# A bound on the transfers in flight in a scan followed by a mixture of adapters

## The chip, the cores and the metric

The kernel runs on one core of a Trainium2 chip. The metric is the device time of one execution in microseconds, as the median of several runs. The profile is of one further execution; its span runs from the first to the last instruction.

## The reference

There are two parts. The first is a linear recurrence over time, for 8 sequences of 6,400 steps with 128 channels: `h = a[:, t] * h + b[:, t]`, and every `h` is kept. The second takes the 51,200 rows of the result, `x`, and adds a mixture of low-rank adapters to each:

```python
logits = x @ w_gate                      # 8 experts
topk = the two largest logits of a row   # w = softmax over these two
delta = sum over both: w * ((x @ A[e]) @ B[e])   # A[e]: 128 x 16, B[e]: 16 x 128
out = x + delta
```

All inputs and outputs are float32. `a` and `b` are 26.2 MB each and are read once; the output is 26.2 MB and is written once.

## The kernel before

The 51,200 rows are cut into 100 units of 512 rows. One unit goes through these steps:

- **Load** (`load`, L533, issued at L350 by SyncE). Rows of `a` and of `b` come in transfers of 512 KB, two units each; the first one of `a`, the first two of `b` and the last one of `a` are single units of 256 KB. Each of the two inputs has a ring of 8 places (`a_in`, `b_in`).
- **Transpose** (`AB`, L571). TensorE turns the rows into channels by time, into PSUM.
- **Scan** (L605, L629). ScalarE copies the transposed `a` to SBUF (`a_st`), and VectorE scans it with the transposed `b`, into `xT` in float16.
- **Products and gates** (`ZL` L668, `zl` L686, and L735 to L824). TensorE multiplies `xT` by the gate weights and all the `A` at once, ScalarE parks the result, and VectorE, GpSimd and ScalarE find the two largest logits and their weights, for three units at a time.
- **Weighting and output** (`mul` L845, `T` L853, `tev` L861, `D` L881, `oev` L896). The products are weighted, turned, multiplied by `B` and added to `x` in PSUM; ScalarE copies the sum into one of 24 output slots (`outt`).
- **Store** (`store`, L913, also issued at L350 by SyncE). Two units, 512 KB, go out in one transfer; the last two units go out singly.

SyncE does nothing but issue these 153 transfers: 51 of `a`, 51 of `b` and 51 stores. The order of the work on every engine is written out ahead by a planner, `_Plan.schedule`. It takes each operation's cost, a key (unit plus an offset for its kind) and its dependencies, and fills `self.order`, one list for each engine. A store has the key of 20 units later (`hold`) and also depends on the scan of that later unit, so that stores are mixed with the loads from the 41st transfer on. After planning, `_Plan.run` walks an engine's list: it waits on semaphores for what the operation depends on (L194), then emits it. Each DMA has a semaphore of its buffer place and counts to 16, one for each DMA engine that has done its part.

Before the change, a transfer waits only for its buffers: a load for the transposes that last read its place, a store for its two units' `oev` and the later scan. Beyond that, SyncE issues as early as it can.

Of the kernel before, what the change touches and what calls it, by code (L numbers as in the profile page):

```python
# [12 lines left out]
CFG = {  # L13
    "ring": 8,
    "xr": 20,
    "zr": 48,
    "nout": 24,
    "hold": 20,
    "heads": (1, 1, 1, 1),
    "group": 3,  # L20
    "tails": (2, 2, 1, 1),
# [20 lines left out]
class _Op:  # L42


    def __init__(self, name, eng, kind, unit, busy, lat, emit, deps, dma, mode, takes, gives):
        self.name = name
        self.engs = (eng,) if isinstance(eng, str) else eng
        self.eng = self.engs[0]
        self.kind = kind
        self.unit = unit  # L50
        self.busy = busy if isinstance(busy, dict) else {e: busy for e in self.engs}
        self.lat = lat
        self.emit = emit
        self.deps = deps
        self.dma = dma
        self.mode = mode
        self.takes = list(takes)
        self.gives = gives
        self.next = None
        self.turn = None  # L60
        self.signal = False
        self.done = None


class _Plan:


    def __init__(self, sems, latency, weight, offset, switch, banks, caps, least):
        self.sems = sems
        self.latency = latency  # L70
        self.weight = weight
        self.offset = offset
        self.switch = switch
        self.banks = banks
        self.caps = caps
        self.least = least
        self.ops = {}
        self.order = {e: [] for e in sems}
        self.bank_of = {}
# [10 lines left out]
    def schedule(self):  # L90
        ops = self.ops
        users = {n: [] for n in ops}
        left = {}
        glued = {op.next for op in ops.values() if op.next}
        for op in ops.values():
            op.deps = [ops[d] for d in dict.fromkeys(op.deps) if d in ops]
            left[op.name] = len(op.deps)
            for d in op.deps:
                users[d.name].append(op)
            op.key = self.weight * (op.unit + self.offset.get(op.kind, 0.0))  # L100
        end = {}
        cand = {e: [] for e in self.sems}
        free = {e: 700.0 for e in self.sems}
        link = 0.0
        mode = None
        idle = [(0.0, i, None) for i in range(self.banks)]
        held = {r: 0 for r in self.caps}
        for op in ops.values():
            if not left[op.name] and op.name not in glued:
                for e in op.engs:  # L110
                    cand[e].append((0.0, op))
        todo = len(ops)
        turn = 0
        while todo:
            best = None
            for e, c in cand.items():
                for x in c:
                    op = x[1]
                    if op.turn is not None and op.turn != turn:
                        continue  # L120
                    t = max(free[e], x[0])
                    takes = op.takes + (ops[op.next].takes if op.next else [])
                    if takes:
                        want = {}
                        for r, _ in takes:
                            want[r] = want.get(r, 0) + 1
                        kept = sum(max(0, k - held[r] - want.get(r, 0)) for r, k in self.least.items())
                        if len(takes) + kept > len(idle) or any(held[r] + k > self.caps[r] for r, k in want.items()):
                            continue
                        t = max(t, idle[len(takes) - 1][0])  # L130
                    if op.mode and mode and op.mode != mode:
                        t += self.switch
                    late = op.busy[e] - min(op.busy.values())
                    if best is None or (t + late, op.key) < best[:2]:
                        best = (t + late, op.key, e, x, t)
            _, _, e, pick, t = best
            for x in pick[1].engs:
                cand[x].remove(pick)
            run = [pick[1]] + ([ops[pick[1].next]] if pick[1].next else [])
            for op in run:  # L140
                for role in op.takes:
                    _, i, giver = idle.pop(0)
                    self.bank_of[role] = i
                    held[role[0]] += 1
                    if giver and giver.eng != e:
                        run[0].deps.append(giver)
            for op in run:
                turn += op.turn is not None
                op.eng = e
                mode = op.mode or mode  # L150
                self.order[e].append(op)
                free[e] = t + op.busy[e]
                t = free[e]
                if op.dma:
                    link = max(link, free[e] + 550.0) + op.dma[2]
                    end[op.name] = link + op.dma[3]
                else:
                    end[op.name] = free[e] + op.lat[e]
                if op.gives:
                    held[op.gives[0]] -= 1  # L160
                    idle.append((end[op.name], self.bank_of[op.gives], op))
                    idle.sort(key=lambda x: x[:2])
                todo -= 1
                for u in users[op.name]:
                    left[u.name] -= 1
                    if not left[u.name] and u.name not in glued:
                        for x in u.engs:
                            cand[x].append((max(end[d.name] for d in u.deps), u))
        self.span = max(end.values())
        for op in ops.values():  # L170
            if op.eng == "pe":
                op.deps = [d for d in op.deps if d.eng != "pe"]
            for d in op.deps:
                d.signal = True
        for e, seq in self.order.items():
            n = 0
            for op in seq:
                if op.dma:
                    op.done = op.dma[:2]
                else:  # L180
                    n += op.signal
                    op.done = (self.sems[e], n)
# [18 lines left out]
def bass_associative_scan_2x2__then__mixture_of_adapters_kernel(  # L201
# [28 lines left out]
    KEY = CFG["key"]  # L230
# [59 lines left out]
    with ExitStack() as stack:  # L290
# [38 lines left out]
        psum = [sb(nc.psum_tensor(f"ps{i}", [128, UT], F32)) for i in range(8)]  # L329
# [4 lines left out]
        sems = {e: sb(nc.semaphore(f"s_{e}")) for e in ("pe", "dve", "act", "pool", "sp")}  # L334
        dma_sem = {}

        latency = {"pe": 205.0, "dve": 170.0, "act": 230.0, "pool": 130.0, "sp": 100.0}
        plan = _Plan(sems, latency, 1000000.0, KEY, 100.0, len(psum), CFG["caps"], CFG["least"])
        add = plan.add

        def add_dma(name, eng, unit, starts, slot, ns, deps=(), kind="dma", issue=450.0, after=2000.0):
# [105 lines left out]
        for name, eng, lo, hi, time in (("spr0", "pool", 0, 3, 900.0), ("spr1", "dve", 3, 8, 760.0)):  # L447
# [10 lines left out]
                    op=ALU.mult,  # L458
# [549 lines left out]
```

## Time and profile before

| | |
|---|---|
| time | 202.24 us, median of 3 runs (202.14 to 203.49) |
| span of the profiled execution | 200.8 us |
| busy: PE, PEld, DVE, ACT, POOL | 90%, 80%, 87%, 89%, 79% |
| moved by DMA | 79.30 MB, mean 395 GB/s |
| a 512 KB transfer, from issue to landing | median 15.2 to 15.4 us |
| mean granted TensorE clock | 0.988 |

PE is TensorE's matmuls, PEld its weight loads, DVE VectorE, ACT ScalarE, POOL GpSimd, SP SyncE; a q behind the name (SPq) stands for the engine's sequencer, which waits and issues. Lines of groups and waits name the tile, the line of the kernel and what was waited for, with the total in us, the number of times and the longest. In the stretches of time the columns are the stretch, its length, the busy time of each engine with its number of instructions, the granted clock, the mean busy share of the 16 DMA engines and GB/s. "Issue" as a cause of waiting means that the profile shows nothing the engine waited for.

### The profile page before, as it was taken

How to read it: one execution, taken by the hardware profiler on the slowest of the kernel's cores; microseconds unless marked ns; L12 is line 12 of the kernel's file. 1: busy time of each engine (PE TensorE's matmuls, PEld its weight loads, DVE VectorE, ACT ScalarE, POOL GpSimd, SP SyncE). 2: the span in 40 equal slices, each digit the busy share in tenths (PEclk: the TensorE clock that was granted, in tenths of full speed). 3: DMA queues.
4: the chain of work that ended last, by engine and by line, in shares of the span. 5: the costliest groups of instructions: out<-in, count | busy, mean ns of one | idle time of the engine just before them, and what ended most of it. 6: DMA issues, size and time to landing. Idle time of an engine off the chain costs nothing.

```text
span 200.8 us, 8186 instructions
## 1 busy us (share of the span) xinstructions
PE 181.6 (90%) x3202; PEld 161.6 (80%) x3202; DVE 174.3 (87%) x302; ACT 179.6 (89%) x463; POOL 158.4 (79%) x278
## 2 busy tenths in 40 slices
PE   7688899997997999999899999999999999989671
PEld 4577788897996888889788999888989889979461
DVE  4389999999899998899998989879889799889980
ACT  3379999999897999999899999999999999999872
POOL 2234749889696988897859999999899998897850
PEclk9889999999999999999999999999999999999998
DMA  6999999999999999999999999999999999985997
GB/s 206 367 419 410 406 409 404 412 403 406 408 418 414 417 412 417 411 417 416 411 414 419 411 415 415 419 415 415 417 417 412 413 415 415 406 340 202 371 406 276
DMA packets 22629, 79.30 MB, mean 395 GB/s; under 512 B 2624, under 2 KB 2880, under 8 KB 22592
## 3 DMA queue, kind: packets, MB, share of 16 engines
q1 hardware_dynamic: 22160, 78.65, 97.6%
q8 instruction: 25, 0.41, 0.8%
q10 hardware_dynamic: 432, 0.14, 0.3%
q14 instruction: 12, 0.10, 0.1%
HBM read 52.56 MB, written 26.21 MB: 392 GB/s over the span
## 4 chain that ended last, share of the span: by engine, by line
PE 47%; DVE 18%; ACT 14%; DMA 7%; issue 6%; SPq 4%; POOL 2%; POOLq 1%; DVEq 0%; ACTq 0%
PE ps L571 17%; PE ps L881 15%; DVE xT L629 13%; PE ps L668 8%; DMA b_in<-in_b_dram 7%; PE ps L853 7%; ACT a_st L605 4%; ACT zl L686 4%; ACT outt L896 4%; SPq L350 4%; DVE zwT L861 2%; ACT pn L735 1%; ACT g L824 1%; DVE zw L845 1%; POOLq L290 1%
## 5 line engine op out<-in xcount | busy, mean ns | idle before, releaser
L629 DVE TENSOR_TENSOR_SCAN xT<-a_st,xT,ps 128x512 f16<-128x512 f32 x96 | 120.4, 1254 | 12.5 <-PE ps L571 4.5
L845 POOL TENSOR_TENSOR zw<-zl,g 128x512 f16<-128x512 f32 x93 | 99.2, 1071 | 10.2 <-ACT g L824 10.1
L686 ACT COPY zl<-ps 128x408 f32<-128x408 f32 (+1 forms) x139 | 74.6, 543 | 1.6 <-PE ps L668 1.4
L571 PE MATMUL ps<-ident_f,a_in 64*128 64x64 f32 (+1 forms) x792 | 68.3, 230 | 4.9 <-DMA a_in<-in_a_dram 2.4
L605 ACT COPY a_st<-ps 128x512 f32<-128x512 f32 x100 | 62.2, 641 | 8.8 <-PE ps L571 8.0
L571 PE MATMUL ps<-ident_f,b_in 64*128 64x64 f32 (+1 forms) x792 | 68.3, 231 | 1.8 <-issue 1.7
L571 PEld LDWEIGHTS ps<-ident_f,a_in 64*128 64x128 f32 (+1 forms) x792 | 57.1, 140 | 14.5 <-issue 5.2
L896 ACT COPY outt<-ps 128x512 f32<-128x512 f32 x100 | 61.8, 633 | 3.2 <-PE ps L881 2.7
L571 PEld LDWEIGHTS ps<-ident_f,b_in 64*128 64x128 f32 (+1 forms) x792 | 57.1, 141 | 1.2 <-issue 1.0
L668 PE MATMUL ps<-cst_h,xT 128*128 128x136 f16 x400 | 50.3, 234 | 0.8 <-DVE xT L629 0.7
L881 PE MATMUL ps<-ident_h,xT 128*128 128x128 f16 x400 | 42.1, 228 | 1.0 <-DVE zwT L861 0.8
L853 PE MATMUL ps<-ident_h,zw 128*128 128x128 f16 x400 | 38.9, 220 | 3.9 <-DVE zw L845 2.0
L881 PE MATMUL ps<-cst_h,zwT 128*128 128x128 f16 x400 | 39.0, 219 | 1.4 <-issue 1.4
L668 PEld LDWEIGHTS ps<-cst_h,xT 128*128 128x128 f16 x400 | 36.2, 148 | 4.6 <-DVE xT L629 1.5
L861 DVE COPY zwT<-ps 128x256 f32<-128x256 f32 x89 | 35.8, 411 | 3.2 <-PE ps L853 3.2
L881 PEld LDWEIGHTS ps<-ident_h,xT 128*128 128x128 f16 x400 | 32.9, 146 | 3.0 <-DVE zwT L861 1.9
L853 PEld LDWEIGHTS ps<-ident_h,zw 128*128 128x128 f16 x400 | 25.0, 98 | 9.0 <-DVE zw L845 3.0
L881 PEld LDWEIGHTS ps<-cst_h,zwT 128*128 128x128 f16 x400 | 27.2, 99 | 0.4 <-issue 0.4
L735 ACT ACTIVATE pn<-d 128x96 f32<-128x96 f32 (+2 forms) x72 | 23.6, 336 | 1.0 <-POOL d L777 0.6
L785 POOL TENSOR_TENSOR L<-zl,pn 128x96 f32<-128x96 f32 (+2 forms) x34 | 12.9, 378 | 6.9 <-ACT pn L735 5.7
L807 POOL TENSOR_TENSOR d<-d 128x96 f32<-128x96 f32 (+2 forms) x36 | 13.8, 383 | 4.3 <-DVE d L760 3.9
L814 POOL TENSOR_TENSOR um<-d,pn 128x96 f32<-128x96 f32 (+2 forms) x36 | 14.0, 388 | 2.8 <-ACT pn L735 1.4
(40 smaller groups left out, 87.7 us busy)
## 6 DMA issues: line engine op xcount, KB each, us to landing
a_in<-in_a_dram SPq DMA_DIRECT2D x49, 512.0 KB, 15.4
b_in<-in_b_dram SPq DMA_DIRECT2D x49, 512.0 KB, 15.3
out_dram<-outt SPq DMA_DIRECT2D x49, 512.0 KB, 15.2
a_in<-in_a_dram SPq DMA_DIRECT2D x2, 256.0 KB, 9.0
b_in<-in_b_dram SPq DMA_DIRECT2D x2, 256.0 KB, 4.4
out_dram<-outt SPq DMA_DIRECT2D x2, 256.0 KB, 2.9
cst_f<-in_moe_A_dram ACTq DMA_DIRECT2D x1, 64.0 KB, 3.2
cst_f<-in_moe_B_dram ACTq DMA_DIRECT2D x1, 64.0 KB, 5.8
```

Of the source, the lines that this page charges most:

```text
L571: last = h.transpose(*args())
L605: lambda h: h.copy(a_st[w % NAS][:, :], bank(("a", w))[:, :]),
L629: last = h.tensor_tensor_scan(out=x_at(lo, hi), data0=a_st[w % NAS][:, lo:hi], data1=bank(("b", w))[:, lo:hi], initial=init, op0=ALU.mult, ...
L668: last = h.matmul(dst, x_block((b0 + j) // Q, (b0 + j) % Q), wA_h)
L686: return h.copy(zl[:, r0 : r0 + n, :], src)
L735: lambda h: h.activation(v(pn[s]), v(src[s]), ACTF.Relu, bias=bias, scale=scale),
L814: lambda h: h.tensor_tensor(out=v(um[s]), in0=v(d1[s]), in1=v(pn[s]), op=ALU.subtract),
L845: lambda h: h.tensor_tensor(out=oview, in0=zview, in1=gview, op=ALU.mult),
L853: last = h.transpose(dst[:, q * 128 : (q + 1) * 128], zw[v % NZW][:, q, :], ident_h[:, :])
L861: return copy(zwT[v % NZT][:, :].bitcast(F32), bank(("O", v))[:, 0 : UT // 2])
L881: last = h.matmul(bank(("O", v))[:, cols], (x_block(v, q), zwT[v % NZT][:, cols])[part], (ident_h[:, :], Bcat_h)[part], start=part == 0 an ...
L896: return copy(outt[:, v % NOUT, :], bank(("O", v))[:, :])
```

## The change

After the planner has settled the order, every transfer of SyncE's list also gets a dependency on the one four places earlier in the same list. SyncE then waits, before it issues a transfer, until that earlier one has landed, so that at most four are in flight, the new one included. The order of the transfers, their sizes, the buffers and all that the other engines do stay as they were. It is meant to keep the queues of the DMA engines short, in place of the twelve or so transfers that stand in them now.

```diff
@@ CFG
     "hold": 20,
+    "flight": 4,
@@ _Plan.__init__
+        self.flight = flight
@@ _Plan.schedule
         self.span = max(end.values())
+        moves = [op for op in self.order["sp"] if op.dma]
+        for old, new in zip(moves, moves[self.flight :]):
+            new.deps.append(old)
         for op in ops.values():
             if op.eng == "pe":
                 op.deps = [d for d in op.deps if d.eng != "pe"]
```

`flight` is handed to the planner where it is made (L338).

More of the change, by code (lines that the diff above doesn't have):

```diff
@@ L65, with __init__ @@
 class _Plan:
-    def __init__(self, sems, latency, weight, offset, switch, banks, caps, least):
+    def __init__(self, sems, latency, weight, offset, switch, banks, caps, least, flight):
         self.sems = sems
@@ L337, in bass_associative_scan_2x2__then__mixture_of_adapters_kernel @@
         latency = {"pe": 205.0, "dve": 170.0, "act": 230.0, "pool": 130.0, "sp": 100.0}
-        plan = _Plan(sems, latency, 1000000.0, KEY, 100.0, len(psum), CFG["caps"], CFG["least"])
+        plan = _Plan(sems, latency, 1000000.0, KEY, 100.0, len(psum), CFG["caps"], CFG["least"], CFG["flight"])
         add = plan.add
```

## The prediction

> **What bounds the kernel now.** I read the page's slices and queue rows first, to see whether the DMA engines have room to lose:
>
> ```profile
> DMA  6999999999999999999999999999999999985997
> q1 hardware_dynamic: 22160, 78.65, 97.6%
> q8 instruction: 25, 0.41, 0.8%
> a_in<-in_a_dram SPq DMA_DIRECT2D x49, 512.0 KB, 15.4
> b_in<-in_b_dram SPq DMA_DIRECT2D x49, 512.0 KB, 15.3
> out_dram<-outt SPq DMA_DIRECT2D x49, 512.0 KB, 15.2
> ```
>
> They have almost none: 97.6% of sixteen engines' time is SyncE's queue. In the trace's landings one 512 KB transfer follows another every 1.25 to 1.28 us, so 15.3 us from issue to landing is 15.3 / 1.26 = 12 transfers in flight. SyncE's timeline shows how the twelve come about:
>
> ```profile
> 9.15 0.43 SPq L350 DMA_DIRECT2D a_in<-in_a_dram  x1
> 9.63 0.43 SPq L350 DMA_DIRECT2D b_in<-in_b_dram  x1
> 10.10 1.98 SPq L350 DMA_DIRECT2D a_in<-in_a_dram  x1
> 12.13 1.05 SPq L350 DMA_DIRECT2D b_in<-in_b_dram  x1
> ```
>
> An issue takes 0.43 us until the queue is full; from 10 us on it takes 1 to 3 us, because the sequencer is stuck inside it. The buffers don't hold SyncE back, the queue does.
>
> Does a late load cost anything? The chain of waits, for the whole span and then from 30 to 185 us:
>
> ```profile
> PE ps L571 <- DMA a_in<-in_a_dram: 2.4, 3, 1.5
> ...
> PE ps L571 <- DMA a_in<-in_a_dram: 0.2, 1, 0.2
> ```
>
> TensorE waits for loads only before 30 us. Up to unit 19 its transposes start 0.05 to 1.2 us after the later of their two loads has landed; from unit 31 on they start 4.7 to 9.7 us after (unit 60: landed 100.43, started 105.83). From then on the busy time by stretches sets the pace (PE, PEld, DVE, ACT, POOL):
>
> ```profile
> 40.00:160.00 120.00, 114.12 (x2112) 104.12 (x2111) 108.74 (x181) 114.40 (x290) 107.64 (x182) 1.00 1.03 414
> 160.00:175.00 15.00, 15.00 (x266) 13.59 (x266) 14.06 (x25) 14.77 (x38) 13.40 (x24) 1.00 1.03 414
> ```
>
> TensorE and ScalarE are busy 95% from 40 to 160 us and 98 to 100% after it. So two resources run level: DMA, 5 us ahead, and TensorE with ScalarE. What still interrupts TensorE is in the list of waits and in the chain that ended last:
>
> ```profile
> PEld ps L571 <- issue: 6.2, 17, 1.2
> PE ps L571 <- issue: 1.7, 2, 1.0
> PE ps L881 <- issue: 1.4, 2, 1.2
> ...
> 49.18 1.04 issue
> 62.94 1.17 issue
> 99.14 0.66 issue
> ```
>
> "Issue" is a wait for nothing that the profile names. Counting TensorE's instructions in the trace, these three stops come after instructions 1473, 1985 and 3265, which are 2 and 5 times 256 apart, and each follows a packet of the q8 instruction queue (47.73 to 48.83, 61.55 to 62.52, 97.41 to 98.48 us). They are stops for TensorE's own program.
>
> **What the Trainium skill says.** "Runtime: NRT & Kernel Launch", section Instruction fetch mechanics: the program is streamed in blocks of 16 KiB, 256 instructions, over a DMA queue that the sequencer drives, and mostly hidden. The trace agrees on the blocks (25 packets, 0.41 MB, is 16 KB each, for 6,404 TensorE instructions) and not wholly on "hidden". "DMA: Bandwidth & Descriptors", Queues, rings and completion order: an engine takes turns between its queues packet by packet. The trace agrees in that a fetch takes about 1.0 us beside two data packets stretched from 0.16 to about 0.44 and 0.38 us. Same page, Anatomy of one DMA: a transfer has a fixed cost near 2.0 us, mostly the receipt. Here a lone 256 KB store lands after 2.9 us; less 0.63 us of moving, that leaves 2.3 us, but the trace puts more of it at the start than at the receipt (below). Same page, Why a DMA increments its semaphore by 16 and not by 1: only the full count says that all engines are done, so the added wait is one for the slowest engine. The sixteen landings of a transfer lie 0.4 us apart at 3 us, 2.9 at 30, 4.1 at 90 and 6.6 at 175.
>
> **The change, part by part.** It adds 149 waits on SyncE (153 transfers less four). It moves no instruction and keeps the order; no other engine gets a wait.
>
> *The wait itself.* Behind the waiting SyncE are only later transfers, so the question is whether the engines run dry. From an engine's last packet to the visible landing the trace has 0.35 to 0.50 us. SyncE's wake-up is not shown; I take 0.1 us, twice the 0.05 us between two free issues (ends 0.05 and 0.3). From issue to the first data packet: 1.0 us for the first load (0.74 to 1.74), 0.75 us for stores near the end (183.35 to 184.1). Round trip: 0.45 + 0.1 + 1.0 = 1.55 us. Meanwhile the slowest engine still holds three transfers, 3 x 1.26 = 3.8 us. It never runs dry; 2.2 us are spare. The end of the run supports this: from 188 to 198 us, with two to four others in flight, stores still land every 1.23 to 1.39 us. Cost: 0.
>
> *The other waits.* A transfer would be issued some 10 us later than now, so its buffer waits (loads on transposes, stores on scans) are older when it gets there: 0. Only the last stores, held for the last scans until 183.35 and 185.34 us, keep today's issue times.
>
> *Coupling the engines.* Now an engine that loses 1.5 us to a fetch (1.0 plus 0.5 of stretched packets; landings at transfers 11 and 57 jump by 1.5) falls behind alone, up to 6.6 us. After the change no engine can be over 2.2 us ahead of the slowest. One fetch fits in that; a second one on the same engine, before the slowest has had one too, costs 2 x 1.5 - 2.2 = 0.8 us. With 24 fetches on 16 engines I reckon six such cases at most, 5 us; the least is 0. The slowest engine has its own jumps in any case (three of 1.1 to 1.5 us now), each of which gives all others room again, so I take 1 us. That lies beside the 4.7 us that loads are early, and 5.3 us between a store's landing and the reuse of its output slot (unit 80: 163.60 and 169.01). At the end the stores leave about 1 us of gaps. Cost on the end: 0 to 4, taken 0.3 us.
>
> *The fetches.* A fetch starts 2.5 to 5.3 us after TensorE has entered the block before. It needs 1.0 us, and TensorE goes on no sooner than 1.3 us after its end. The stops of 1.04, 1.17 and 0.66 us belong to starts after 5.1 to 5.3 us; at 2.5 to 3.5 us there is no stop. Part of that delay should be the data packets that the engine has already taken in. Now about 12 x 8 = 96 packets stand at an engine; after, 32 at most (5 us), and on an engine that leads by 2.2 us about 18. Gain if fetches start 1.4 us sooner: all the stops at block ends, 1.04 + 1.17 + 0.66 + 0.4 of smaller ones = 3.3 us, nearly all on the chain. If the delay isn't the queue: 0. I take half, 1.6 us, since the slowest engines keep some 28 packets.
>
> Sum: 202.24 + 0.3 - 1.6 = 200.9 us.
>
> **The rivals.** *Nothing happens*: the fetches' delay is their own, the engines' order is the same. For it: packets are shared in turns, so depth alone need not matter. 202.24 + 0.3 = 202.5. *All stops go*, and the early stretch gains too: before unit 20 every load is waited for, transfers 2 and 3 land 1.7 us later than the rate allows, and transfer 11 loses 1.5 us to a fetch. With fewer transfers issued at once some of that may not occur: 202.24 + 0.3 - 3.3 - 0.5 = 198.7. Against it: transfers 2 and 3 are issued as before. *Coupling wins*: fetches fall on leading engines and the spare 2.2 us is smaller under load, so SyncE adds bubbles; 5 us of delay, less 1 us of gaps, gives 202.24 + 4 = 206.2, the case that is slower. Against it: the round trip is measured on both sides, and most of the middle is hidden.
>
> **How the numbers follow.** Forecast 0.44, nothing 0.20, all stops 0.20, coupling 0.16. A forecast that lies 0.7 us above the mark of 1% (200.2) falls below it in somewhat over a third of its cases: faster 0.20 + 0.17 = 0.37. Slower by 1% (over 204.3) is the coupling and a remnant of "nothing": 0.17. The rest, 0.46, is within 1%. The range runs from the whole stop gain, 198.8, to half-way into the coupling case, 204.8.
>
> **What would show it.** Right: time from issue to landing near 5 us for all three kinds; issues of 0.4 us; DMA still 9 in the slices up to 175 us; a transfer's sixteen landings never over about 2.3 us apart; shorter "issue" waits of L571. Wrong towards slower: slices of DMA at 7 or 8 in the middle, waits of L571 on a_in after 40 us, loads ending well after 176 us. Wrong towards no effect: the 1 us "issue" stops still there. A first load phase that ends at another time than before would mean that I mis-sized the start.

## The result, and the profile after

The kernel with the bound takes 221.88 us (median of 4 runs, 218.67 to 224.09) against 202.31 us before: ratio 1.083, 95% interval 1.074 to 1.092. The forecast was 200.9 us, range 198.8 to 204.8. The kernel is slower, and by some four times the 4 us that my slower rival allowed. (Two of the four runs count as slow, so the ratio rests on the other two, 218.67 and 219.94 us, and is below 221.88 / 202.31.)

Of the page before, the GB/s of the slices and the chain that ended last, by engine:

```profile
GB/s 206 367 419 410 406 409 404 412 403 406 408 418 414 417 412 417 411 417 416 411 414 419 411 415 415 419 415 415 417 417 412 413 415 415 406 340 202 371 406 276
...
PE 47%; DVE 18%; ACT 14%; DMA 7%; issue 6%; SPq 4%; POOL 2%; POOLq 1%; DVEq 0%; ACTq 0%
```

The page of the changed kernel, first the slices (DMA busy in tenths, GB/s), then the chain, then the transfers with their time from issue to landing:

```profile
DMA  5999999999999999989999999999999999999995
GB/s 203 377 402 349 348 397 376 364 383 368 373 361 390 350 381 305 387 305 354 393 373 392 376 376 366 386 311 394 367 340 373 383 376 374 377 390 401 400 406 219
...
DMA 55%; PE 17%; ACT 10%; DVE 7%; issue 3%; POOL 3%; POOLq 1%; SPq 1%; DVEq 0%
...
a_in<-in_a_dram SPq DMA_DIRECT2D x49, 512.0 KB, 5.6
b_in<-in_b_dram SPq DMA_DIRECT2D x49, 512.0 KB, 5.6
out_dram<-outt SPq DMA_DIRECT2D x49, 512.0 KB, 5.5
```

The bound does what it says: 5.6 us to landing, three others in flight at every issue. But look at its first two lines together. The engines still read 9 in nearly every slice, while the bytes that they move fall below 380 GB/s in many of them. The busy share hides most of this loss, because a packet that takes longer counts as busy for longer (such packets are counted below); GB/s shows it. The chain, which led through DMA for 7% of the span before, is now 55% DMA. By stretches (columns as before):

```profile
0.00:40.00 40.00, 33.14 (x499) 26.32 (x501) 31.62 (x53) 28.69 (x76) 18.58 (x44) 0.96 0.93 350
40.00:160.00 120.00, 109.08 (x1997) 99.54 (x1995) 104.11 (x171) 110.00 (x277) 103.69 (x175) 0.99 0.99 365
```

From 40 to 160 us it is 365 GB/s in place of 414, while the busy share falls only from 1.03 to 0.99 (above 1, the packets overlap a little in the record). And TensorE waits for loads again, all through the run; the list of waits of the changed kernel (L576 is L571 of before) has:

```profile
PEld ps L576 <- DMA b_in<-in_b_dram: 12.0, 16, 2.7
PEld ps L576 <- DMA a_in<-in_a_dram: 11.6, 16, 1.6
PE ps L576 <- DMA b_in<-in_b_dram: 9.1, 12, 2.5
PE ps L576 <- DMA a_in<-in_a_dram: 8.3, 14, 1.4
```

The landings in the trace tell where the time went. The last load lands at 193.76 us in place of 175.96, 17.8 us later, and the last store at 217.62 in place of 200.25, 17.4 later. From transfer 4 to 132 there are 128 intervals between landings. Those that are more than 0.1 us above 1.26 us are above it by 23.0 us in sum, in 36 intervals, in place of 5.5 us in 12. So it isn't a slower steady rate: 85 of the 128 still last between 1.20 and 1.36 us, and 36 jumps make up the loss. The loads' lead over TensorE still grows to 7 us at unit 34, but is eaten up by unit 47, which starts 0.2 us after its load; from there on the loads set the pace.

### The profile page after: what moved, and what is told of

It is laid out like the page before. It is cut to its first block, busy times and chain, and to the rows that moved or that the text cites. A ratio compares the mean times of both kernels' runs of the same rounds, so it can differ in the third digit from the quotient of the medians.

```text
span 218.2 us, 8276 instructions
## 1 busy us (share of the span) xinstructions
PE 184.4 (85%) x3202; PEld 163.1 (75%) x3202; DVE 175.8 (81%) x302; ACT 182.0 (83%) x463; POOL 158.8 (73%) x278
## 4 chain that ended last, share of the span: by engine, by line
DMA 55%; PE 17%; ACT 10%; DVE 7%; issue 3%; POOL 3%; POOLq 1%; SPq 1%; DVEq 0%
DMA b_in<-in_b_dram 27%; DMA a_in<-in_a_dram 23%; PE ps L576 7%; DMA out_dram<-outt 5%; DVE xT L634 5%; PE ps L886 5%; ACT zl L691 3%; PE ps L673 3%; PE ps L858 3%; ACT outt L901 3%; ACT a_st L610 2%; ACT pn L740 1%; POOL zw L850 1%; DVE zw L850 1%; POOLq L295 1%
## 5 line engine op out<-in xcount | busy, mean ns | idle before, releaser
L576 PE MATMUL ps<-ident_f,a_in 64*128 64x64 f32 (+1 forms) x792 | 69.8, 230 | 19.0 <-DMA b_in<-in_b_dram 9.1
L576 PEld LDWEIGHTS ps<-ident_f,a_in 64*128 64x128 f32 (+1 forms) x792 | 57.2, 140 | 30.5 <-DMA b_in<-in_b_dram 12.0
L610 ACT COPY a_st<-ps 128x512 f32<-128x512 f32 x100 | 60.9, 619 | 19.9 <-PE ps L576 18.7
L691 ACT COPY zl<-ps 128x408 f32<-128x408 f32 (+1 forms) x139 | 71.2, 520 | 1.0 <-PE ps L673 0.9
L576 PE MATMUL ps<-ident_f,b_in 64*128 64x64 f32 (+1 forms) x792 | 69.8, 230 | 0.1
L901 ACT COPY outt<-ps 128x512 f32<-128x512 f32 x100 | 60.3, 614 | 3.5 <-PE ps L886 2.3
L576 PEld LDWEIGHTS ps<-ident_f,b_in 64*128 64x128 f32 (+1 forms) x792 | 57.1, 140 | 0.3 <-issue 0.2
L886 PE MATMUL ps<-ident_h,xT 128*128 128x128 f16 x400 | 42.6, 230 | 0.7 <-DVE zwT L866 0.6
L858 PE MATMUL ps<-ident_h,zw 128*128 128x128 f16 x400 | 39.8, 224 | 3.2 <-DVE zw L850 2.1
L886 PEld LDWEIGHTS ps<-ident_h,xT 128*128 128x128 f16 x400 | 33.4, 147 | 2.3 <-DVE zwT L866 1.4
L858 PEld LDWEIGHTS ps<-ident_h,zw 128*128 128x128 f16 x400 | 25.8, 100 | 6.7 <-DVE zw L850 3.1
L740 ACT ACTIVATE pn<-d 128x96 f32<-128x96 f32 (+2 forms) x72 | 22.1, 314 | 0.7 <-POOL d L782 0.6
L812 POOL TENSOR_TENSOR d<-d 128x96 f32<-128x96 f32 (+2 forms) x36 | 13.7, 381 | 3.7 <-DVE d L765 3.2
```

What stands on the lines that cost most here:

```text
L576: last = h.transpose(*args())
L610: lambda h: h.copy(a_st[w % NAS][:, :], bank(("a", w))[:, :]),
L691: return h.copy(zl[:, r0 : r0 + n, :], src)
L740: lambda h: h.activation(v(pn[s]), v(src[s]), ACTF.Relu, bias=bias, scale=scale),
L858: last = h.transpose(dst[:, q * 128 : (q + 1) * 128], zw[v % NZW][:, q, :], ident_h[:, :])
L886: last = h.matmul(bank(("O", v))[:, cols], (x_block(v, q), zwT[v % NZT][:, cols])[part], (ident_h[:, :], Bcat_h)[part], start=part == 0 an ...
```

## The experiments

**How far the bound has to be loosened.** Only the number is changed.

```diff
-    "flight": 4,
+    "flight": 5,
```

> All 148 added waits stay, only the bound is five in place of four. Theory A (round trip): from the changed kernel's trace a new transfer reaches an idle engine 0.36 us (receipt) + 0.06 us (wake-up) + about 2.1 us (issue to first packet) = 2.5 us after the slowest engine finished the transfer it waited for, so an engine can be ahead of the slowest by (flight - 1) x 1.26 - 2.5 us: 1.3 us at four, less than the 1.5 us that an instruction fetch costs an engine; 2.5 us at five. Fetches are mostly absorbed again: 203 to 209 us. Theory B (the waits themselves on SyncE cost time, whatever their distance): still 216 to 222 us. Theory C (every transfer that is issued later lands later, in proportion to the depth given up): a fall by about 2 to 3 us for each step of flight, 217 us.

Measured: 203.38 us, ratio to the kernel before 1.003 (1.001 to 1.006).

> Bound six. Theory A: an engine may be 3.8 us ahead, two fetches' worth: 200 to 204 us. If the shorter stops for instructions are worth something by themselves, it shows here: up to 3 us under the kernel before. Theory B: 216 to 222 us. Theory C: about 214 us.

Measured: 202.67 us, ratio 1.001 (0.998 to 1.003).

> Bound eight. Theory A: 6.3 us ahead, no fetch is felt: 199.5 to 203 us. Theory B: 216 to 222 us. Theory C: about 209 us.

Measured: 203.38 us, ratio 1.003 (1.001 to 1.005).

> Bound twelve, about what the queue holds by itself: the waits are all there and hardly ever hold SyncE. Theory A and C: the time of the kernel before, 201 to 203.5 us. Theory B: 216 to 222 us.

Measured: 203.49 us, ratio 1.003 (1.000 to 1.005).

One transfer more gives back nearly all of the 8%. The added waits cost about 0.3% (B falls: with five, 140 of the 148 held transfers are still issued within 0.1 us of the landing that they waited for), and there is no slope from depth to time (C falls). The page of the kernel with a bound of five:

```profile
GB/s 212 381 418 411 400 363 405 405 404 404 408 416 410 411 419 413 398 394 413 405 408 408 414 412 410 406 407 418 398 383 381 390 408 391 416 412 383 409 392 161
...
a_in<-in_a_dram SPq DMA_DIRECT2D x49, 512.0 KB, 6.4
```

Mostly above 400 again with 6.4 us to landing. These runs also answer the question of the stops for instructions. The "issue" pieces in the chain of the kernel with a bound of six, the longest of its first 100 us:

```profile
48.17 1.18 issue
62.07 1.17 issue
...
98.55 0.69 issue
```

They come at nearly the same times as before and are about as long (1.04, 1.17 and 0.66 us there), at half the depth. With five there are two of them, 0.91 and 1.17 us. With four none is longer than 0.7 us, but there TensorE is held up by loads, so that it can reach the ends of its blocks later.

**The transfers by themselves.** To see whether four is too few by itself, the compute is left out: SyncE walks the same list, waiting only for the transfer `flight` places back (the stores write zeros), and TensorE either does nothing or streams matmuls on a constant tile, which makes it fetch program and nothing else.

```diff
-            plan.run("sp", h)
+            plan.moves_only(h, ready)
...
+            for i in range(CFG["stream"]):
+                h.matmul(psum[i // 16 % 8][:, 0:128], warm_t[:, 0:128], warm_t[:, 0:128])
```

> Only SyncE's 153 transfers in their order, bound of four, no buffer waits; all compute is left out (stores write zeros), so TensorE fetches no program. Theory A (a bound of four is too tight only because fetches displace single engines): nothing pushes engines apart, three transfers' work (3.8 us) covers the round trip of 2.5 us, landings 1.26 to 1.28 us apart, 193 to 198 us. Rival D (four in flight is by itself too few for this round trip, fetches or not): landings on average 1.38 us apart, 210 to 218 us.

Measured: 205.54 us.

> The same with a stream of 3,202 TensorE matmuls on a constant tile, which fetch as many program blocks as the kernel's and wait for nothing. Theory A: 24 or so fetches of 1.5 us on engines that lead by no more than 1.3 us: the 0.5 to 0.9 us lost at each come back, 207 to 216 us, with a jump of the landings at each fetch. Rival D: as without the stream, within 3 us.

Measured: 219.75 us, about the whole kernel's time with a bound of four (218.67 and 219.94 us), with none of its compute.

> The same stream with the bound at twelve. Theory A: fetches fall on engines that may lead by more than 10 us, only the unluckiest engine's own count: 195 to 201 us. Rival D: the same, 195 to 201 us; but then the gap to four without the stream is as large as to four with it.

Measured: 199.89 us. With four in flight the fetches add 219.75 - 205.54 = 14.2 us; with fetches, the step from twelve to four costs 219.75 - 199.89 = 19.9 us. But moves alone came 7.5 us above the most that I had expected of them, so a control was needed:

> Moves only, no stream, bound of twelve: the control for moves only at four (205.5 us). Theory A in its strict form (only program fetches push engines apart): 195 to 198 us, and the 8 to 10 us between it and four have another cause, such as slow single packets that are seen in the trace of four after 60 us (0.3 to 2.2 us each). If those slow packets occur here too and cost nothing, the coupling is to any loss on one engine, not to fetches alone. Rival D: no such packets here, 195 to 198 us as well, but then the difference to four is spread evenly over the transfers.

Measured: 195.89 us. Thus four costs 9.6 us even without program fetches, and theory A in its strict form falls. (The two ran on different chips; the kernel before took 202.98 us on the one and 204.00 on the other, which is small beside 9.6.) The stretches of moves only with four, then with twelve (the last column is GB/s):

```profile
10.00:40.00 30.00, 3.93 (x1) 0.00 (x0) 1.00 1.02 405
60.00:170.00 110.00, 0.00 (x0) 0.00 (x0) 1.00 1.00 382
```

```profile
10.00:40.00 30.00, 3.93 (x1) 0.00 (x0) 1.00 1.03 411
60.00:170.00 110.00, 0.00 (x0) 0.00 (x0) 1.00 1.03 419
```

With loads alone and no fetches four in flight is nearly enough: from 20 to 50 us the trace has a landing every 1.25 to 1.30 us, but for one of 1.47. Stores are issued from 50 us on, and after that there are jumps of up to 2.5 us, so rival D (too few always, spread evenly) falls as well. What the jumps consist of shows in the 4 KB packets. At the line rate one takes 0.159 us; this counts those over 0.3 us after 12 us of each trace, and what they took above 0.159 us, summed over all engines:

| kernel | packets over 0.3 us | excess, us |
|---|---|---|
| before | 58 | 14.5 |
| changed, four | 492 | 218.5 |
| five / six / eight | 144 / 81 / 58 | 55.8 / 26.1 / 15.0 |
| moves only, twelve | 2 | 0.4 |
| moves only, four | 243 | 121.6 |
| moves and fetches, twelve | 42 | 10.8 |
| moves and fetches, four | 528 | 246.9 |

In the changed kernel 218.5 us over 16 engines is 13.7 us for each, against 0.9 before. The slow packets, up to 2.1 us long, aren't program fetches; they are data packets, and nearly all such packets are quick when twelve transfers stand in the queue. The remainder is engines with nothing to do: from 12 to 193 us fewer than 16 packets are under way in 26% of the time, 5.3 us for each engine, where before, from 12 to 175 us, it is never so. Together that is 18 to 19 us, about the 17.8 us by which the last load is late. A slow packet starts among idle engines more often than a quick one: just before its start fewer than 16 packets are under way in half of the cases (40 to 160 us), against 23% for packets below 0.2 us. The packets carry no engine number, though, so that each slow packet is a restart isn't shown.

> Moves and a stream of 1,601 matmuls of 256 columns in place of 3,202 of 128: half the program blocks, so 12 to 13 fetches over about the same stretch, bound of four. Theory A: the cost goes with the number of fetches, about half of the 14 us between 205.5 (none) and 219.8 us (25 fetches): 210 to 215 us. Rival F (a busy TensorE slows the transfers, whatever it fetches): 217 to 222 us.

```diff
-    "stream": 3202,
+    "stream": 1601,
...
-                h.matmul(psum[i // 16 % 8][:, 0:128], warm_t[:, 0:128], warm_t[:, 0:128])
+                h.matmul(psum[i // 16 % 8][:, 0:256], warm_t[:, 0:128], warm_t[:, 0:256])
```

Measured: 214.46 us with 12 fetches, between 205.54 with none and 219.75 with 25. The loss goes with the fetches: the first twelve cost 8.9 us and the other thirteen 5.3, which is no firm difference, since the two runs with none lie 2.5 us apart and this one is of another chip. TensorE is busy for 177 us here, against 182 with 25 fetches, so rival F falls.

> Moves and the full stream, bound of five. Theory A: room of 2.5 us, 25 fetches mostly absorbed: 200 to 205 us. Rival D and F: 210 us or more.

Measured: 199.56 us, no more than with twelve; 97 slow packets in place of 528.

**The round trip.**

> Moves only, bound of one: each transfer waits for the one before it, nothing else is under way. The spacing is the round trip plus 1.26 us. With the numbers of my prediction (0.45 + 0.1 + 1.0 for loads, 0.45 + 0.1 + 0.75 for stores) 2.8 us for loads and 2.6 for stores, 420 us in all. If the round trip of 2.5 us seen with four in flight is the same when nothing else is under way, 3.8 us and 570 us.

Measured: 477.29 us in one run, between the two. The transfers of this run, with the time from issue to landing:

```profile
a_in<-in_a_dram SPq DMA_DIRECT2D x49, 512.0 KB, 3.5
b_in<-in_b_dram SPq DMA_DIRECT2D x49, 512.0 KB, 3.2
out_dram<-outt SPq DMA_DIRECT2D x49, 512.0 KB, 2.6
```

In its trace the next issue follows a landing after 0.02 us, and the first packet follows the issue after 0.96 us for loads and 0.84 for stores. These are the parts that I had. A store then needs 2.62 - 0.84 - 0.36 = 1.4 us for its data, which is the line rate and a little. A load needs 3.18 - 0.96 - 0.36 = 1.9 us or, of `a`, 2.2: among the first packets of a load many are slow (1,022 packets over 0.3 us in this run, all but one of them in loads). So the missing part of the round trip should be the first read from HBM, and stores, which read SBUF, should be free of it. That was still a guess:

> 152 loads of 512 KB and one store, with the stream of 25 fetches, bound of four; all compute is left out. Theory G (an engine that has run dry restarts with a packet whose read from HBM is not hidden, 0.3 to 2.3 us in place of 0.16): loads suffer in full, some 500 or more packets over 0.3 us, 214 to 226 us. Rival H (the restart is paid in issue and receipt, which loads and stores share; the read is not the point): loads and stores lose the same, 8 to 20 us each, against their own twelve.

> The same with twelve: control, 196 to 202 us, under 100 packets over 0.3 us, in both theories.

> 153 stores of 512 KB with the stream, bound of four. A store read from SBUF has its first packet 0.84 us after issue and no slow first packet when alone (landing after 2.62 us, of which 1.4 for the data). Theory G: round trip 0.36 + 0.02 + 0.84 = 1.2 us, room 3.8 - 1.2 = 2.6 us, over the 1.5 us of a fetch: within 3 us of the control with twelve, few packets over 0.3 us. Rival H: 8 to 20 us over the control.

> The same with twelve: control. If writes to HBM keep the rate of the end of the kernel before (1.23 to 1.39 us each), 195 to 213 us, in both theories.

```diff
+        for i, (dst, src, sem, value) in enumerate(moves):
+            if i >= self.flight:
+                handle.wait_ge(*moves[i - self.flight][2:])
+            handle.dma_start(dst, src).then_inc(sem, 16)
```

Measured: loads 233.08 us with four and 218.90 with twelve; stores 223.17 with four and 222.86 with twelve. (All four begin some 14 us late, behind the clearing of the output tile, so only the differences count.) The stretch from 20 to 200 us of the four, in the order loads four, loads twelve, stores four, stores twelve:

```profile
20.00:200.00 180.00, 161.56 (x2894) 161.38 (x2891) 0.00 (x0) 0.00 (x0) 0.96 0.98 369
```

```profile
20.00:200.00 180.00, 161.38 (x2891) 161.21 (x2888) 0.00 (x0) 0.00 (x0) 0.96 1.03 408
```

```profile
20.00:200.00 180.00, 161.96 (x2901) 161.79 (x2898) 0.00 (x0) 0.00 (x0) 0.96 0.99 393
```

```profile
20.00:200.00 180.00, 161.98 (x2902) 161.80 (x2898) 0.00 (x0) 0.00 (x0) 0.96 1.02 404
```

Loads lose 14.2 us, stores 0.3, under the same number of fetches. Slow packets are 476 against 72 for loads and 58 against 83 for stores: they belong to loads, as theory G has it. But the equal ends of the stores say less than they seem to. In both runs one of a transfer's sixteen landings falls behind the other fifteen from the start (with twelve it ends at 220.6 us, the others by 214.8) and sets the end by itself, so what the other engines lose doesn't show in the time. In the stretch shown, stores with four do run 3% below those with twelve.

The changed kernel's own trace decides between G and H, with loads and stores under the same bound and the same fetches. From the ninth transfer on, take those whose first landing tells that an engine was free early: the first landing of the transfer before, less 0.38 us of receipt, came less than 1.7 us after the issue. Of 31 such loads 23 leave a gap, which is to say that their own first landing follows the one before by more than 1.37 us, where 1.27 us is the time for the data. Of 32 such stores 4 do. A cost in issue and receipt would hit both; H falls.

The levels of the four runs missed what was expected: loads with twelve ended 16.9 us above the most, stores with twelve 9.9, and I had left out the late start. The comparison is between four and twelve of a kind, so the late start doesn't touch it.

**An attempt that settles nothing.** Each transfer in two halves of 64 partitions, each half held for its own half four transfers back (of the edit, the line for loads; stores are split alike):

```diff
-                [(dst, src)],
+                [(dst[c : c + 64], src[c : c + 64]) for c in (0, 64)],
```

> The whole kernel, each transfer issued as two of 64 partitions, each half with its own semaphore and each held for the same half four transfers back: the same 2 MB in flight, in eight pieces of 0.63 us. Theory A: the room is 7 x 0.63 - 2.5 = 1.9 us in place of 1.3, over the 1.5 us of one fetch: 204 to 211 us. Rival E (it is the 2 MB in flight that counts, bytes over latency): 217 to 222 us as with four whole ones. If halves are slower by themselves, the time is above 222 us and says nothing without its own control.

Measured: 274.16 us. Its stretch of loads shows why:

```profile
20.00:40.00 20.00, 15.22 (x188) 12.93 (x187) 10.92 (x15) 11.83 (x33) 6.05 (x15) 0.59 1.03 234
```

The kernel before has in the same stretch:

```profile
20.00:40.00 20.00, 18.74 (x363) 16.54 (x360) 19.36 (x28) 19.31 (x51) 14.76 (x29) 1.00 1.03 408
```

With the engines as busy, only 234 GB/s move in place of 408, so it looks like a matter of the halves themselves; without a control of its own it says nothing on the bound.

## Why the prediction was wrong

**What bounds the kernel** was read rightly, with DMA nearly full and the loads some 5 us ahead of TensorE. So was the form of the danger: the rival "coupling wins" named engines that fall behind one at a time and a spare that shrinks under load.

**"Round trip: 0.45 + 0.1 + 1.0 = 1.55 us ... It never runs dry; 2.2 us are spare ... Cost: 0."** This is the step that failed. Receipt, wake-up and first packet measure 0.36, 0.02 to 0.06 and 0.96 us, as I put them or better. But I set the first packet's start equal to full rate from then on, and so put the wait for the first data of a load at nothing. In the changed kernel 46 of 94 loads leave a gap as above; their first landing comes a median of 3.7 us after issue. Less 1.27 us of data and 0.38 us of receipt that is 2.0 us (1.3 to 2.8), not 1.0. This is an estimate from landings, which don't name their engine: it holds any slow packet of the load, and by the same sum the engine still had other work until a median of 1.7 us after the issue, and was without for the last 0.3 us or so. That the extra time belongs to loads is shown by the 23 of 31 loads against 4 of 32 stores; that it is the first read from HBM is the reading that fits, not one that a run isolates. The round trip is then 0.38 + 0.06 + 2.0 = 2.4 us and the room 3.8 - 2.4 = 1.4 us, just below the 1.5 us that one fetch takes. So the engines do run dry: 5.3 us for each. With five in flight the room is 2.6 us by the same sum, and the loss is gone. The stores at the end of the run, which I called as evidence for four, have no such first read: I carried a number from stores to loads. The first load's 1.0 us was a start of packets only. (The section Anatomy of one DMA of "DMA: Bandwidth & Descriptors", which I cited from the Trainium skill for a fixed cost near 2.0 us, describes transfers issued by GpSimd. These are issued by SyncE, and no term of the sum came from it.)

**"Coupling the engines ... Cost on the end: 0 to 4, taken 0.3 us."** Measured 17.4 us at the last landing. Two terms were too small. I let six of 24 fetches be felt, 5 us at most; in the moves alone 25 fetches add 14.2 us. And without any fetch four still costs 9.6 us against twelve, with slow data packets of up to 2.3 us. I had no term for that. As I read it, a held engine restarts with such packets, and they hold the others in turn; the trace shows that slow packets and idle engines come together, not which causes which. The 5 us that I allowed is about the lead that the loads have over TensorE; 17.8 us couldn't hide behind it.

**"The fetches ... I take half, 1.6 us"** of gain. It isn't there. From five to twelve in flight the two long stops are still there, 0.9 to 1.2 us as before, so the depth of the queue isn't what makes them. "Nothing happens" was the right case for this part.

**"The other waits: 0"** and the cost of the waits as instructions held: a bound of five keeps 148 of the 149, nearly all of which still hold SyncE, and costs 0.3%.

**My signs** were mixed. Time to landing near 5 us (5.5 to 5.6) and issues of 0.4 us (0.33) came as listed; waits on `a_in` after 40 us and loads ending late gave the slower case away. "Slices of DMA at 7 or 8" did not: they stayed at 9, since slow packets count as busy. Nor did the sixteen landings of a transfer stay within 2.3 us: in 41 of 153 transfers they lie further apart, 3.3 us at most. Two details of the working don't come out: the whole gain from stops gives 202.24 + 0.3 - 3.3 = 199.2 us, not 198.8, and one of the stores from 188 to 198 us lands 1.65 us after the one before it. Neither bears on the miss.

What stays open is why a packet of a load takes 0.3 us at one time and 2 us at another, and what disturbs the moves alone once the stores have begun.

## What to carry to other kernels

A bound on transfers in flight needs room for the round trip and, on top of it, for the longest hiccup that a single DMA engine can have. For the round trip, take the time until the data of a load flow while other transfers are under way, not the time to the first packet and not that of stores. These runs fit this sum but don't make it exact: four in flight lost time even without the hiccups that I had counted. Here five transfers of 512 KB were enough and four weren't, and keeping the queue that short gained nothing over twelve. When DMA is suspected, read GB/s and not only the busy share, and count the slow packets. And when two variants end at the same time, look whether one engine alone sets that end: it can hide what the others lose.

## What the runs showed of the hardware

- In the changed kernel the data of a load flowed some 2.0 us after its issue, where a gap shows it (an estimate from the landings of 46 loads, 1.3 to 2.8). With one transfer at a time the first packet comes 0.96 us after the issue of a load, and its data take 1.9 to 2.2 us; for a store it is 0.84 us and 1.4 us.
- In this mix of loads and stores a bound of four turned 58 slow packets into 492. With loads alone it turned 72 into 476; with stores alone there were 58, against 83 with twelve.
- The busy share of the DMA engines is no measure of their rate: at a share of 0.99 they moved 365 GB/s, at 1.03 it was 414.
- A 16 KB program fetch takes 0.9 to 1.1 us on one DMA engine of the kernel before and moves it back by 1.5 us, while the others go on (the landings of transfers 11 and 57 come 1.5 us late, those between them on time).
- With stores alone and twelve in flight, the latest of the sixteen landings came every 1.34 us, the one before it every 1.30 us (transfers 10 to 140).
- Loads in halves of 64 partitions moved 234 GB/s from 20 to 40 us, against 408 in the kernel before, with the engines as busy.
